# Halves of the heads in batch 0's attention, and a list of units over eight steps instead of four

## The chip, the cores and the metric

The kernel runs on one core of one Trainium2 chip. What counts is the time of one execution on the device in microseconds. Three runs of the kernel before took 1492.59 to 1493.74 us, 1492.81 in the median. One further execution was profiled. It took 1490.52 us, and the span that its trace covers is 1488.7 us. The mean clock granted to TensorE over that span is 0.992 of full speed. The engines are called PE (TensorE), DVE (VectorE), ACT (ScalarE), POOL (GpSimd) and SP (SyncE, which issues the DMAs here).

## The reference

Eight batches and eight heads attend twice, first with 32 packed queries over the keys, then with all queries over the packed result. Two feed-forward networks follow.

```python
# q, k, v: (8, 8, 576, 64), p: (8, 8, 32, 64); w_a, w_b: (512, 1536); w_out: (1536, 512)
# second network: w_in (512, 2048), w_out (2048, 512)
def sm_attn(qq, kk, vv):
    s = 0.125 * np.matmul(qq, kk.transpose(0, 1, 3, 2))
    a = np.exp(s - np.max(s, axis=-1, keepdims=True))
    a = a / (np.sum(a, axis=-1, keepdims=True) + 1e-09)
    return np.matmul(a, vv)
p_packed = sm_attn(p, k, v)
out = sm_attn(q, p_packed, p_packed)
x = out.transpose(0, 2, 1, 3).reshape(4608, 512)
x = (x @ w_a) * (x @ w_b) @ w_out
h = x @ w_in2
x = (h * np.clip(h + 3.0, 0.0, 6.0) / 6.0) @ w_out2
```

## The kernel before

**Numbers.** Every FP32 product of the two networks is made of three matmuls over high and low parts (`mm3`, L90 to L92): high by high, high by low, low by high. A high part is a copy of a value in the matmul's type, made on ACT as a rule, and the low part is the difference, made on DVE or POOL. All weights come as 64-bit words and are turned into FP32 in pieces of 128x512: `ld` loads a piece, `sq` (L112) and `lw` (L115, the low words, written into the destination) run on ACT, `a0` (L119), `a1` (L123) and `a2` (L128) on DVE, `a3` (L131) merges on POOL, and `st` stores the result to DRAM for later use. `sq 3` is that operation of piece 3. A scratch array of a piece is `cv_ap` in the trace, its raw words `f64p`, and the finished weights of a step `rab`.

**Phase 1** runs in 48 steps: 4 groups of two batches by 12 steps, one for each block of 128 columns of the first network's inner dimension. The attention's second product is never formed by itself: step t multiplies the packed attention `lhs` of both batches into the weights (`pw`, 16 matmuls, L524). `pwh` on ACT (L532) and `pwl` on DVE (L536) split its two PSUM banks into `pw_hi` and `pw_lo`. Then `ab t b h` multiplies them with the second softmax `at_hi`, `at_lo` (12 matmuls into two PSUM tiles, once for each of two batches and two halves of the tokens). `aba` (ACT, L564) copies one of the two tiles out, `abg` (DVE, L570) multiplies it with the other to `g`, `gh` (ACT, L577) and `gl` (POOL, L581) split it. Every third step makes 16 `y` units ready, of 9 matmuls each, which multiply three steps of `g` by `wo_hi`, `wo_lo` (`woh` on ACT, `wol` on POOL) and add the result to an accumulator.

**Attention units of a batch**, in order: `s1` (first scores, 16 matmuls over two banks, L214), `s1c` (copy to `ex`), `mx` (maximum), `ex` (exponential, L240), `et` and `et2` (transposes on PE, L246 and L259), `etc` and `et2c` (their copies on ACT, L251 and L264), `rs`, `pv` (40 matmuls, L280), `pp` (scaling, L287), `bd` (transpose) and `bdc` (copy into `lhs`). Then the second scores `s2`, their 32x32 transposes `s2c` (L309), `mx2`, `su2`, `ex2`, `sm2`, `mu2` (L333), `tr2` (L337), `ath` (ACT, L346) and `atl` (L350, on POOL, `atld` on DVE). The two digits behind a name are the batch and `c`, one of two arrays that hold four heads each; `s1`, `s1c`, `s2` and `s2c` take the half of the tokens instead. A `d` or `p` at the end of a name puts the unit on DVE or POOL.

**The order.** Every engine runs its instructions in the order in which the program issues them. For the first `TO` steps this order is the text `OPENING`, unit by unit. From step `TO` on a loop issues a step's `pw`, its `ab` units and `y` units with background units spread between them: the attention of later batches, from number `N_BG` of their list on, and the conversions. Units put off with `later` come due after a number of ticks; `DUE` holds what is still put off when the list ends. PSUM has eight banks: three tagged `att`, two `y`, three `ab`. In the opening a unit that asks for a bank takes them in rotation, from the token `bank` on as its own tag says. The second phase (the second network) is not touched.

Of the kernel before, what the change touches and what calls it, by code (L numbers as in the profile page):

```python
# [44 lines left out]
v 1 0, s2 0 0, ex 1 0, lw 2, ld, q 1 0, s2 0 1, s2c 0 0, s2c 0 1, a1 2, mx2 0 0, su2 0 0, mx2 0 1, q 1 1, a2 2, ex 1 1,
ex2 0 0, et 1 1, su2 0 1, etc 1 1, et 1 0, et2 1, ex2 0 1, ld, a0 3, etc 1 0, et2c 1, sm2 0 0, pv 1, a3 2, sm2 0 1, mu2 0 0,
rs 1, mu2p 0 1, sq 3, pp 1, tr2 0 0, tr2 0 1, bd 1, lw 4, bdc 1, a1 3, s2 1 0, s2c 1 0, ld, pw 0, st 1, lw 3, a0 4, st 2,
ath 0 1, ath 0 0, atl 0 1, a1 4, pwh 0 0, atl 0 0, pwl 0 0, pwh 0 1, pwl 0 1, s2 1 1, ab 0 0 0, s2c 1 1, mx2 1 0, mx2 1 1,
su2 1 0, a2 3, su2d 1 1, ab 0 0 1, a3 3, aba 0 0, ex2 1 0, abg 0 0, ex2 1 1, gh 0 0, sm2 1 0, pw 1, gl 0 0, aba 0 1, sq 4,
pwh 1 0, ld, abg 0 1, sm2 1 1, a2 4, mu2 1 1, gh 0 1, pwh 1 1, pwl 1 0, pwl 1 1, mu2p 1 0, a3 4, tr2 1 1, ab 1 0 0, ab 1 0 1,  # L50
aba 1 0, tr2 1 0, gl 0 1, abg 1 0, ys 0 1, ath 1 1, ath 1 0, ld, ys 0 0, atld 1 0, lw 5, aba 1 1, atl 1 1, gh 1 0, ab 0 1 0,
gl 1 0, sq 5, aba 0 2, abg 1 1, a0 5, ab 0 1 1, p 2, k 2 1, abg 0 2, v 2 0, st 3, a1 5, bank, gh 1 1, ld, gl 1 1, aba 0 3,
gh 0 2, abg 0 3, gl 0 2, gh 0 3, a0 6, a2 5, gl 0 3, sq 6, k 2 0, q 2 0, s1 2 0, s1c 2 0, s1 2 1, ys 0 3, v 2 1, a3 5, a1 6,
st 5, lw 6, s1c 2 1, ys 1 1, a2 6, mx 2 0, a0 7, mx 2 1, a1 7, sq 7, ld, ys 1 0, lw 7, sq 8, pw 2, a2 7, a3 6, ys 0 2,
ex 2 0, pwh 2 1, q 2 1, st 4, et 2 0, pwh 2 0, a0 8, pwl 2 0, lw 8, ex 2 1, a3 7, etc 2 0, pwl 2 1, a1 8, a2 8, lw 9,
ab 1 1 0, a3 8, aba 1 2, a0 9, woh 0 0, et 2 1, ld, abg 1 2, sq 9, gh 1 2, ld, etc 2 1, a1 9, ab 1 1 1, aba 1 3, abg 1 3,
wol 0 0, a2 9, et2 2, p 3, st 7, ab 2 0 0, ld, woh 0 1, st 8, wol 0 1, aba 2 0, st 6, gl 1 2, sq 10, abg 2 0, a3 9, rs 2,
et2c 2, a0 10, ys 1 2, woh 1 0, pv 2, pp 2, ld, a1 10, woh 1 1, bd 2, bdc 2, a0 11, pw 3, wol 1 0, gh 2 0, gl 2 0, st 9,
lw 10, ab 2 0 1, a2 10, pwh 3 0, lw 12, aba 2 1, ab 2 1 0, aba 2 2, ld, ys 2 0, abg 2 1, a3 10, gh 2 1, pwh 3 1, wol 1 1,
a1 11, pwl 3 0, woh 2 0, abg 2 2, wol 2 0, sq 12, woh 2 1, st 10, gh 1 3, pwl 3 1, a0 12, wol 2 1, ld, ld, gl 2 1, gl 1 3, y,  # L60
a1 12, ys 2 1, k 3 0, gh 2 2, gl 2 2, sq 11, a2 11, lw 11, a3 11, ab 2 1 1, ys 2 2, aba 2 3, a2 12, y, s2 2 0, y, ys 1 3,
abg 2 3, st 11, gh 2 3, a3 12, lw 13, ld, s2c 2 0, a0 13, ab 3 0 0, k 3 1, ab 3 0 1, ld, s2 2 1, s2c 2 1, aba 3 0, abg 3 0,
y, gh 3 0, a1 13, sq 13, gl 3 0, pw 4, gl 2 3, ys 2 3, v 3 1, aba 3 1, pwh 4 1, abg 3 1, v 3 0, a0 14, lw 14, y, a1 14,
# [1186 lines left out]
```

## Time and profile before

| | |
|---|---|
| median of three runs | 1492.81 us (1492.59 to 1493.74) |
| profiled execution | 1490.52 us |
| its span | 1488.7 us |
| PE busy | 1446.8 us, 97% of the span |
| DVE busy | 1089.7 us, 73% |
| ACT busy | 714.9 us, 48% |
| POOL busy | 561.6 us, 38% |
| DMA | 231 GB/s in the mean |

An engine's busy time counts the instructions that the profile times, not its waits. The idle time before an instruction is put down to the engine and line whose semaphore came last. A share of busy time is a mean over stretches with different limits, so the stretches have to be looked at one by one. The start of the span stands apart: only there the conversion of weights, the first attention units and the first steps compete for DVE, ACT and POOL at once.

### The profile page before, as it was taken

To read this page: it belongs to the slowest core of one execution; us is meant where nothing else is said; L and a number is where in the kernel's file an instruction comes from. 1 tells how busy PE (TensorE), PEld (TensorE's weight loads), DVE (VectorE), ACT (ScalarE), POOL (GpSimd) and SP (SyncE) were. 2 spreads that over 40 slices of the span, in tenths; PEclk is the share of its full clock that TensorE was granted. 3 is DMA by queue.
4 is the path that set the end of the run, shared out by engine and by line. 5 is a ranking of instruction groups with operands and counts; after the bars stand their busy time and mean duration, and the time that the engine had idled before them with its cause. 6 is when DMAs were issued, how large, how long until landed. Compare 5 with 4: busy or idle time off the path is not lost.

```text
span 1488.7 us, 29158 instructions
## 1 busy us (share of the span) xinstructions
PE 1446.8 (97%) x11416; PEld 1378.3 (93%) x11416; DVE 1089.7 (73%) x1728; ACT 714.9 (48%) x1421; POOL 561.6 (38%) x552
## 2 busy tenths in 40 slices
PE   4898999999999999999999999999999999999998
PEld 2687898999999899999999999999999999999998
DVE  5987785677865678535447788788788788878777
ACT  4665655565555555454423443453443343353333
POOL 2676555575554655645630324024024022111000
PEclk8899999999999999999999999999999999999999
DMA  9675545655577543855428768778768777867755
GB/s 313 222 232 169 174 155 204 225 195 181 180 245 229 168 167 134 272 200 185 178 75 333 286 248 314 270 265 309 283 232 298 290 257 291 298 221 292 267 217 184
DMA packets 120106, 344.54 MB, mean 231 GB/s; under 512 B 11424, under 2 KB 50336, under 8 KB 108192
## 3 DMA queue, kind: packets, MB, share of 16 engines
q1 hardware_dynamic: 119968, 342.67, 65.1%
q8 instruction: 90, 1.47, 0.4%
q14 instruction: 48, 0.39, 0.1%
HBM read 280.76 MB, written 61.87 MB: 230 GB/s over the span
## 4 chain that ended last, share of the span: by engine, by line
PE 87%; DVE 4%; DMA 3%; POOL 2%; issue 2%; ACT 1%; SPq 0%; DVEq 0%; POOLq 0%; ACTq 0%
PE o L91 8%; PE o L92 8%; PE o L90 8%; PE y L90 7%; PE y L92 6%; PE y L91 6%; PE ab L90 6%; PE ab L92 6%; PE ab L91 6%; PE pw L524 3%; DMA f64p<-in_wab 2%; PE s L214 1%; DMA w<-w2d 1%; POOL wo_lo L510 1%; DVE pw_lo L536 1%
## 5 line engine op out<-in xcount | busy, mean ns | idle before, releaser
L90 PE MATMUL ab<-at_hi,pw_hi 128*128 128x288 f32 x768 | 233.2, 304 | 2.7 <-DVE g L570 1.3
L90 PE MATMUL y<-g_hi,wo_hi 128*128 128x288 f32 x768 | 231.8, 302 | 1.3 <-ACT wo_hi L506 0.7
L92 PE MATMUL ab<-at_hi,pw_lo 128*128 128x288 f32 x768 | 228.6, 298 | 2.3 <-DVE pw_lo L536 2.3
L91 PE MATMUL ab<-at_lo,pw_hi 128*128 128x288 f32 x768 | 228.3, 297 | 0.0
L91 PE MATMUL y<-g_lo,wo_hi 128*128 128x288 f32 x768 | 227.1, 296 | 0.5 <-POOL g_lo L581 0.5
L92 PE MATMUL y<-g_hi,wo_lo 128*128 128x288 f32 x768 | 226.7, 295 | 0.6 <-POOL wo_lo L510 0.6
L91 PE MATMUL o<-ol,wo 128*128 128x384 f32 x672 | 226.9, 338 | 0.2 <-DVE ol L980 0.2
L92 PE MATMUL o<-oh,wo 128*128 128x384 f32 x672 | 226.8, 337 | 0.0
L90 PE MATMUL o<-oh,wo 128*128 128x384 f32 x672 | 225.5, 336 | 0.0
L581 POOL TENSOR_TENSOR g_lo<-g,g_hi 128x288 fp32r<-128x288 f32 x192 | 164.3, 860 | 137.1 <-ACT g_hi L577 133.1
L570 DVE TENSOR_TENSOR g<-a,ab 128x288 f32<-128x288 f32 x192 | 85.9, 447 | 117.0 <-PE ab L92 82.8
L90 PEld LDWEIGHTS y<-g_hi,wo_hi 128*128 128x128 f32 x768 | 144.6, 188 | 19.3 <-DVE acc L614 7.2
L90 PEld LDWEIGHTS ab<-at_hi,pw_hi 128*128 128x128 f32 x768 | 145.8, 190 | 17.3 <-issue 7.2
L718 POOL TENSOR_TENSOR yl_B<-raw_y,yh_B 128x384 fp32r<-128x384 f32 x36 | 50.1, 1412 | 262.8 <-PE h_7y L92 228.7
L92 PEld LDWEIGHTS ab<-at_hi,pw_lo 128*128 128x128 f32 x768 | 145.9, 190 | 3.0 <-DVE pw_lo L536 3.0
L91 PEld LDWEIGHTS ab<-at_lo,pw_hi 128*128 128x128 f32 x768 | 146.0, 190 | 0.1
L92 PEld LDWEIGHTS y<-g_hi,wo_lo 128*128 128x128 f32 x768 | 144.6, 188 | 1.1 <-POOL wo_lo L510 1.1
L91 PEld LDWEIGHTS y<-g_lo,wo_hi 128*128 128x128 f32 x768 | 144.6, 188 | 0.7 <-POOL g_lo L581 0.7
L564 ACT COPY a<-ab 128x288 f32<-128x288 f32 x192 | 76.6, 399 | 125.3 <-PE ab L92 124.6
L577 ACT CAST g_hi<-g 128x288 fp32r<-128x288 f32 x192 | 83.5, 435 | 91.5 <-DVE g L570 91.3
L91 PEld LDWEIGHTS o<-ol,wo 128*128 128x128 f32 x672 | 126.2, 188 | 0.7 <-DVE ol L980 0.5
L90 PEld LDWEIGHTS o<-oh,wo 128*128 128x128 f32 x672 | 126.1, 188 | 0.0
(434 smaller groups left out, 3414.5 us busy)
## 6 DMA issues: line engine op xcount, KB each, us to landing
wo<-wo2d SPq DMA_DIRECT2D x84, 1024.0 KB, 5.7
w<-w2d SPq DMA_DIRECT2D x47, 1280.0 KB, 8.1
w<-w2d SPq DMA_DIRECT2D x47, 512.0 KB, 4.9
rab<-wabf SPq DMA_DIRECT2D x36, 512.0 KB, 5.8
f64p<-in_wo SPq DMA_DIRECT2D x28, 512.0 KB, 3.7
w2d<-w SPq DMA_DIRECT2D x8, 1792.0 KB, 6.7
f64p<-in_wab SPq DMA_DIRECT2D x24, 512.0 KB, 4.9
k<-in_kT SPq DMA_DIRECT2D x16, 576.0 KB, 6.8
```

The lines of the kernel that those rows point to most:

```text
L90: pe.matmul(ps, lhsT=l_hi, rhs=r_hi, start=first, stop=False, skip_group_check=skip)
L91: pe.matmul(ps, lhsT=l_hi, rhs=r_lo, start=False, stop=False, skip_group_check=skip)
L92: pe.matmul(ps, lhsT=l_lo, rhs=r_hi, start=False, stop=last, skip_group_check=skip)
L214: pe.matmul(ps[c][o, :SH], lhsT=lhsT[r, q, :], rhs=kq_t[n, b, q // 2][r, q % 2, ts], start=True, stop=True)
L510: pool.tensor_sub(ol, ro_t[t][:, c * 256:(c + 1) * 256], f32(oh))
L524: pe.matmul(ps[c][o, b, :], lhsT=l[r, b, q, :], rhs=w[r, q, :], start=True, stop=True)
L536: dve.tensor_sub(lo[:, c], ps[c], f32(hi[:, c]))
L564: act.copy(a, ab_t[t, r][0])
L570: dve.tensor_mul(g32, a, p1)
L577: act.copy(g_t[t, r][0], g_t[t, r][2])
L581: pool.tensor_sub(lo, g32, f32(hi))
L718: pool.tensor_sub(lo[:, k], get(n)[:, k], f32(hi[:, k]))
```

## The change

The list covers steps 0 to 7 instead of 0 to 3, and its first part is written in another order. Of the entries that are common to both, many change places; line numbers of the kernel rise with the added functions (L214 becomes L233, L246 L265 and so on).

```diff
-TO, N_BG = 4, 23
-DUE = [[2, ('ys', 3, 3)]]
+TO, N_BG = 8, 43
+DUE = [[1, ('gh', 7, 3), ('gl', 7, 3), ('yslater', 7, 3)]]
 OPENING = """
-ld, k 0 0, p 0, lw 0, k 0 1, p 1, k 1 1, s1 0 0, v 0 1, s1c 0 0, s1 0 1, ld, s1c 0 1, mx 0 0, a0 0, mx 0 1, k 1 0, v 0 0,
...
+k 0 0, ld, p 0, k 0 1, s1x 0 0 0, ld, lw 0, s1x 0 0 1, s1x 0 1 0, p 1, s1x 0 1 1, s1cx 0 0 0, a0 0, s1cx 0 0 1, a1 0, wm,
+s1cx 0 1 0, s1cx 0 1 1, mx 0 0, ex 0 0, k 1 1, mx 0 1, wm, k 1 0, ex 0 1, v 0 0, v 0 1, wm, q 0 0, s1 1 1, et2x 0 1, et 0 1,
...
+    def heads1(ps, lhsT, n, b, h, c):
+        ts = slice(h * SH, (h + 1) * SH)
+        for q in range(4):
+            r, o = slice(64 * c, 64 * c + 64), slice(NP * q, NP * q + NP)
+            pe.matmul(ps[o, :SH], lhsT=lhsT[r, q, :], rhs=kq_t[n, b, q // 2][r, q % 2, ts], start=True, stop=True)
+
+    def s1x(b, h, c):
+        state(b)["s1", h, c] = ps = bank(f"s1_{b}{h}{c}")
+        heads1(ps, p_t[b], "k", b, h, c)
...
+    def et2x(b, c):
+        z = state(b)
+        z["pe", c] = ps = bank(f"et2{b}{c}")
+        for i in range(2):
+            pe.transpose(ps[:TR, i * P:(i + 1) * P], z["ex"][c][:, 3 * P + i * TR:3 * P + (i + 1) * TR], ident)
...
+    def pvx(b, c):
+        z = state(b)
+        z["pv", c] = ps = bank(f"pv{b}{c}")
+        for i in range(5):
+            r = P if i < 3 else TR
+            for q in range(4):
+                pe.matmul(ps[NP * q:NP * q + NP, :64], lhsT=z["et"][c][:r, i, NP * q:NP * q + NP],
+                          rhs=v_t[b, c][:r, i, 64 * q:64 * q + 64], start=i == 0, stop=i == 4)
...
+    def bdx(b, c):
+        z = state(b)
+        z["pb", c] = ps = bank(f"bd{b}{c}")
+        m = 64 if c == 0 else P
+        pe.transpose(ps[:m, :P], z["pp"][:, :m], ident)
...
+    def s2x(b, h, c):
+        z = state(b)
+        z["s2", h, c] = ps = bank(f"s2_{b}{h}{c}")
+        heads1(ps, z["bd"], "q", b, h, c)
...
+    def wm():
+        ps = bank(f"wm{n_bank[0]}")
+        for _ in range(5):
+            pe.transpose(ps[:, :P], ident, ident)
```

`s1x`, `s1cx`, `et2x`, `et2cx`, `rsx`, `pvx`, `ppx`, `bdx`, `bdcx`, `s2x` and `s2cx` are the units of the same name without the x, cut to one `c`, each with a PSUM bank of its own. The list uses them for batch 0 alone; batch 1 keeps the old units. `wm` transposes `ident` five times into a bank that nothing reads; the list holds six. Further added functions, `mx2h` to `atlh` by halves of the tokens and `pwb`, `pwhb`, `pwlb` by batch, are in no list.

On ACT, in the opening of batch 0: `ex` is the exponential, `rab` the low words, `cv_sqp` the squares, `et` the copies of the transposes. Before:

```order
L240 ACTIVATE ex_116,sm_150<-ex_116,nb_136 128x576
L112 ACTIVATE cv_sqp_0_156<-f64p_0_89 128x512
L115 ACTIVATE rab_95<-f64p_1_130 128x512
L240 ACTIVATE ex_117,sm_164<-ex_117,nb_142 128x576
L112 ACTIVATE cv_sqp_1_166<-f64p_1_130 128x512
L251 COPY et_169<-et_152 128x384
L251 COPY et_183<-et_171 128x384
L264 COPY et_169<-et_186 96x256
```

Now, at the same place:

```order
L330 ACTIVATE ex_123,sm_142<-ex_123,nb_140 128x576
L330 ACTIVATE ex_127,sm_158<-ex_127,nb_148 128x576
L131 ACTIVATE cv_sqp_0_193<-f64p_0_91 128x512
L341 COPY et_207<-et_203 128x384
L134 ACTIVATE rab_104<-f64p_1_102 128x512
L341 COPY et_210<-et_187 128x384
L263 COPY et_207<-et_197 96x256
L263 COPY et_210<-et_184 96x256
```

The two exponentials follow each other, and the low words of the second piece stand between the copies.

On DVE, the rows up to the first `pw_lo`: `at` (L337, after L427) are batch 0's last transposes, `cv_ap` the conversion, `t` (L309, after L399) the transposes of batch 1's second scores. Before:

```order
L337 STREAM_TRANSPOSE at_423<-t_317 128x576
L337 STREAM_TRANSPOSE at_425<-t_319 128x576
L123 SCALAR_TENSOR_TENSOR cv_ap_1_354<-f64p_1_303,cv_ap_1_354 128x512
L309 STREAM_TRANSPOSE t_443<-s_100_433 128x288
L309 STREAM_TRANSPOSE t_445<-s_101_434 128x288
L119 TENSOR_SCALAR cv_ap_0_471<-f64p_0_352 128x512
L123 SCALAR_TENSOR_TENSOR cv_ap_0_471<-f64p_0_352,cv_ap_0_471 128x512
L536 TENSOR_TENSOR pw_lo_468<-pw_0_449,pw_hi_467 128x512
L536 TENSOR_TENSOR pw_lo_468<-pw_1_450,pw_hi_467 128x512
```

Now:

```order
L142 SCALAR_TENSOR_TENSOR cv_ap_1_386<-f64p_1_283,cv_ap_1_386 128x512
L138 TENSOR_SCALAR cv_ap_0_474<-f64p_0_335 128x512
L427 STREAM_TRANSPOSE at_476<-t_351 128x576
L427 STREAM_TRANSPOSE at_478<-t_337 128x576
L142 SCALAR_TENSOR_TENSOR cv_ap_0_474<-f64p_0_335,cv_ap_0_474 128x512
L399 STREAM_TRANSPOSE t_517<-s_100_507 128x288
L399 STREAM_TRANSPOSE t_519<-s_101_508 128x288
L672 TENSOR_TENSOR pw_lo_503<-pw_0_484,pw_hi_502 128x512
L672 TENSOR_TENSOR pw_lo_503<-pw_1_485,pw_hi_502 128x512
```

Two conversion instructions stand in front of batch 0's transposes instead of behind them, and one directly behind.

On DVE around the `pw_lo` of step 6, with `g` the products of step 5. Before:

```order
L570 TENSOR_TENSOR g_5_0_1693<-a_0_1691,ab_01_1684 128x288
L119 TENSOR_SCALAR cv_ap_2_1703<-f64p_2_1423 128x512
L123 SCALAR_TENSOR_TENSOR cv_ap_2_1703<-f64p_2_1423,cv_ap_2_1703 128x512
L128 SCALAR_TENSOR_TENSOR cv_ap_2_1703<-cv_sqp_2_1700,cv_ap_2_1703 128x512
L119 TENSOR_SCALAR cv_ap_0_1741<-f64p_0_1504 128x512
L570 TENSOR_TENSOR g_5_1_1763<-a_1_1761,ab_11_1754 128x288
L536 TENSOR_TENSOR pw_lo_1728<-pw_0_1709,pw_hi_1727 128x512
L536 TENSOR_TENSOR pw_lo_1728<-pw_1_1710,pw_hi_1727 128x512
```

Now:

```order
L734 TENSOR_TENSOR g_5_0_1779<-a_0_1737,ab_01_1730 128x288
L142 SCALAR_TENSOR_TENSOR cv_ap_2_1719<-f64p_2_1350,cv_ap_2_1719 128x512
L147 SCALAR_TENSOR_TENSOR cv_ap_2_1719<-cv_sqp_2_1697,cv_ap_2_1719 128x512
L672 TENSOR_TENSOR pw_lo_1762<-pw_1_1744,pw_hi_1761 128x512
L427 STREAM_TRANSPOSE at_1807<-t_1222 128x576
L734 TENSOR_TENSOR g_5_1_1809<-a_1_1804,ab_11_1772 128x288
L138 TENSOR_SCALAR cv_ap_0_1834<-f64p_0_1542 128x512
L142 SCALAR_TENSOR_TENSOR cv_ap_0_1834<-f64p_0_1542,cv_ap_0_1834 128x512
L147 SCALAR_TENSOR_TENSOR cv_ap_0_1834<-cv_sqp_0_1740,cv_ap_0_1834 128x512
L672 TENSOR_TENSOR pw_lo_1762<-pw_0_1743,pw_hi_1761 128x512
```

The half 1 of `pw_lo` stands in front of `g_5_1`, the half 0 five rows behind the first.

## Rows read from the trace of the kernel before

**Rows 1.** The page: engine, busy us, share of the span, instructions.

```profile
PE 1446.8 (97%) x11416; PEld 1378.3 (93%) x11416; DVE 1089.7 (73%) x1728; ACT 714.9 (48%) x1421; POOL 561.6 (38%) x552
```

**Rows 2.** Stretch, length, busy PE, PEld, DVE, ACT, POOL, clock, DMA, GB/s.

```profile
22.00:60.00 38.00, 26.60 (x310) 19.68 (x310) 34.14 (x67) 19.84 (x43) 21.17 (x18) 0.73 0.73 249
60.00:120.00 60.00, 54.75 (x585) 48.04 (x586) 54.57 (x84) 42.53 (x102) 42.30 (x38) 1.00 0.69 227
120.00:140.00 20.00, 16.09 (x144) 13.12 (x144) 13.09 (x22) 11.43 (x27) 14.91 (x15) 0.91 0.54 175
140.00:1488.00 1348.00, 1339.56 (x10227) 1292.54 (x10225) 982.23 (x1542) 631.56 (x1231) 481.14 (x477) 1.00 0.65 231
```

**Rows 3.** Time line, batch 0: start, us, engine, operation, [wait before it <-releaser].

```profile
8.99 2.15 PE L214 MATMUL s<-k,p 64*32 64x288 f32 x24 [0.22 <-DMA k<-in_kT]
...
14.43 0.67 ACT L115 ACTIVATE rab<-f64p 128x512 int32<-128x512 uint16 x1 [0.33 <-DMA f64p<-in_wab]
15.01 0.76 ACT L240 ACTIVATE ex<-ex,nb 128x576 f32<-128x576 f32 x1
16.33 1.00 ACT L251 COPY et<-et 128x384 f32<-128x384 f32 x2
16.61 1.06 PE L259 MATMUL et<-ident,ex 128*96 128x128 f32 x4
17.71 0.64 ACT L264 COPY et<-et 96x256 f32<-96x256 f32 x2 [0.37 <-PE et L259]
...
19.70 1.80 PE L280 MATMUL pv<-v,et 128*32 128x64 f32 x80
21.57 0.48 DVE L287 TENSOR_SCALAR pp<-pv,rs 128x64 f32<-128x64 f32 x2 [4.40 <-PE pv L280]
...
25.83 0.87 PE L246 MATMUL et<-ident,ex 128*128 128x128 f32 x6 [1.77 <-ACT ex L240]
```

**Rows 4.** Time line: a conversion on DVE alone and beside POOL's `at_lo`.

```profile
13.66 0.68 DVE L123 SCALAR_TENSOR_TENSOR cv_ap<-f64p,cv_ap 128x512 uint32<-128x512 uint32 x1
...
36.80 3.00 POOL L350 TENSOR_TENSOR at_lo<-at,at_hi 128x576 fp32r<-128x576 f32 x2 [2.08 <-ACT at_hi L346]
...
38.54 1.80 DVE L123 SCALAR_TENSOR_TENSOR cv_ap<-f64p,cv_ap 128x512 uint32<-128x512 uint32 x1
```

**Rows 5.** Time line of DVE in front of the second `pw_lo`.

```profile
48.67 0.63 DVE L128 SCALAR_TENSOR_TENSOR cv_ap<-cv_sqp,cv_ap 128x512 f32<-128x512 f32 x1
49.21 0.74 DVE L333 TENSOR_TENSOR t<-t,sm 128x576 f32<-128x576 f32 x1
49.87 1.28 DVE L536 TENSOR_TENSOR pw_lo<-pw,pw_hi 128x512 fp32r<-128x512 f32 x2
```

**Rows 6.** DVE's `at_lo`, and its waits (us, times, longest), 44 to 60 us.

```profile
53.54 1.28 DVE L350 TENSOR_TENSOR at_lo<-at,at_hi 128x576 fp32r<-128x576 f32 x1
...
DVE g L570 <- PE ab L92: 1.5, 2, 0.8
```

**Rows 7.** Time line around `ab 4 0`, each matmul by itself.

```profile
100.41 0.29 PE L90 MATMUL y<-g_hi,wo_hi 128*128 128x288 f32 x1
...
103.33 0.44 DVE L570 TENSOR_TENSOR g<-a,ab 128x288 f32<-128x288 f32 x1
...
103.99 0.30 PE L90 MATMUL ab<-at_hi,pw_hi 128*128 128x288 f32 x1
```

**Rows 8.** Time line around the `pw` of step 6.

```profile
122.97 1.07 PE L524 MATMUL pw<-rab,lhs 64*32 64x256 f32 x24 [1.63 <-POOL rab L131]
124.09 1.08 ACT L532 CAST pw_hi<-pw 128x512 fp32r<-128x512 f32 x2 [1.80 <-PE pw L524]
...
127.51 0.46 DVE L570 TENSOR_TENSOR g<-a,ab 128x288 f32<-128x288 f32 x1 [1.97 <-ACT a L564]
128.71 0.71 PE L214 MATMUL s<-k,p 64*32 64x288 f32 x14 [2.28 <-DVE pw_lo L536]
```

**Rows 9.** Busy time and clock by stretch, columns as in rows 2.

```profile
130.00:134.00 4.00, 4.00 (x21) 4.00 (x20) 2.05 (x5) 3.27 (x8) 2.99 (x4) 0.58 0.57 189
```

More of the change, by code (lines that the diff above doesn't have):

```diff
@@ L45 @@
[L45 to L63, printed above, removed]
@@ L338, in tr2, with half, mx2h, su2h @@
         at32_t[b, c] = a
+    def half(x, h):
+        return x[:, 9 * h:9 * h + 9]
+    def mx2h(b, c, h):
+        z = state(b)
+        z["mx"][c, h] = att.tile([P, 9], F32, tag=f"mxh{h}", name=f"mxh{b}{c}{h}", bufs=2)
+        dve.tensor_reduce(z["mx"][c, h], half(z["t"][c], h), axis=AX.X, op=ALU.max)
+    def su2h(b, c, h, on=None):
+        t, m = half(state(b)["t"][c], h), state(b)["mx"][c, h]
+        (on or pool).tensor_tensor(t, t, m.unsqueeze(2).to_broadcast([P, 9, NP]), op=ALU.subtract)
+    def ex2h(b, c, h):
+        t = half(state(b)["t"][c], h)
+        act.activation(t, t, AF.Exp, scale=QK_SCALE)
+    def sm2h(b, c, h):
+        z = state(b)
+        z["sm2", c, h] = s = att.tile([P, 9], F32, tag=f"smh{h}", name=f"smh{b}{c}{h}", bufs=2)
+        dve.tensor_reduce(s, half(z["t"][c], h), axis=AX.X, op=ALU.add)
+        dve.tensor_scalar_add(s, s, 1e-9)
+        dve.reciprocal(s, s)
+    def mu2h(b, c, h, on=None):
+        t, s = half(state(b)["t"][c], h), state(b)["sm2", c, h]
+        (on or dve).tensor_tensor(t, t, s.unsqueeze(2).to_broadcast([P, 9, NP]), op=ALU.mult)
+    def tr2h(b, c, h):
+        if h == 0:
+            at32_t[b, c] = att.tile([P, S], F32, tag="at32", name=f"at32{b}{c}", bufs=2)
+        dve.transpose(at32_t[b, c][:, h * SH:(h + 1) * SH], half(state(b)["t"][c], h).rearrange("p j n -> p (j n)"))
+    def athh(b, c, h):
+        if b not in at_t:
+            at_t[b] = (
+                main.tile([P, 2, S], F32R, tag="at_hi", name=f"at_hi{b}", bufs=3),
+                main.tile([P, 2, S], F32R, tag="at_lo", name=f"at_lo{b}", bufs=3),
+            )
+        ts = slice(h * SH, (h + 1) * SH)
+        act.copy(at_t[b][0][:, c, ts], at32_t[b, c][:, ts])
+    def atlh(b, c, h, on=None):
+        hi, lo = at_t[b]
+        ts = slice(h * SH, (h + 1) * SH)
+        (on or pool).tensor_sub(lo[:, c, ts], at32_t[b, c][:, ts], f32(hi[:, c, ts]))
     def ath(b, c):
@@ L536, in pwl, with pwb, pwhb, pwlb @@
         dve.tensor_sub(lo[:, c], ps[c], f32(hi[:, c]))
+    def pwb(t, b):
+        l = lhs[t // NM1]
+        w = rab_t[t].rearrange("p (q n) -> p q n", q=4)
+        if t not in pw_t:
+            ps = [bank(f"pw{t}_{c}").rearrange("p (b n) -> p b n", b=2) for c in range(2)]
+            pw_t[t] = [
+                main.tile([P, 2, 2, 256], F32R, tag="pw_hi", name=f"pw_hi{t}", bufs=2),
+                main.tile([P, 2, 2, 256], F32R, tag="pw_lo", name=f"pw_lo{t}", bufs=2), ps,
+            ]
+        ps = pw_t[t][2]
+        for q in range(4):
+            for c in range(2):
+                r, o = slice(64 * c, 64 * c + 64), slice(NP * q, NP * q + NP)
+                pe.matmul(ps[c][o, b, :], lhsT=l[r, b, q, :], rhs=w[r, q, :], start=True, stop=True)
+    def pwhb(t, b, c):
+        hi, lo, ps = pw_t[t]
+        act.copy(hi[:, c, b], ps[c][:, b])
+    def pwlb(t, b, c):
+        hi, lo, ps = pw_t[t]
+        dve.tensor_sub(lo[:, c, b], ps[c][:, b], f32(hi[:, c, b]))
+    def wm():
+        ps = bank(f"wm{n_bank[0]}")
+        for _ in range(5):
+            pe.transpose(ps[:, :P], ident, ident)
     def pw_unit(t):
```

80 lines of the change are left out of this document (75 added, 5 removed).

## The prediction

> **What bounds the kernel now.** I read the page's busy times first, then busy time by stretch, then the time lines of the stretches in which PE waits. PE is busy 1446.8 of 1488.7 us [rows 1], so at most 41.9 us of waiting can go, plus what PE loses at its lower clock. The stretches say where it lies [rows 2]: from 140 us on PE is busy 1339.6 of 1348 us, so whatever moves PE earlier in the first 140 us reaches the end unchanged, and nothing behind that point has much to give. From 22 to 60 us PE waits 11.4 us, from 60 to 120 us 5.3, from 120 to 140 us 3.9. DVE is busy 34.1 of 38 us in the first of these and 54.6 of 60 in the second: up to 120 us PE mostly waits for what DVE has not yet done. So in each part I ask what brings DVE forward, or what takes away a stall of PE at 120 to 130 us. Work that only fills a gap of PE is worth nothing by itself.
>
> **The change, part by part.** The DVE, ACT and POOL work is the same set but for two moves (C, D); PE gets 30 transposes more, the six `wm`. Only batch 0 goes through the new half units: batch 1 still uses `s1`, `et2`, `pv` and `s2`. DVE's rows from number 246 on are identical in both orders, so nothing behind step 8 is touched. The new OPENING leaves the same conversions, loads and attention units done at step 8 as the loop did.
>
> *A, up to batch 0's `pp`.* Before, ACT reads low words (0.67, after 0.33 of waiting for a transfer) between the two exps, and the second starts at 15.01; now it follows the first, over 1 us earlier [rows 3]. But PE runs 15 `wm` transposes in front. Four transposes take 1.06 there, 0.27 each. The last score unit ends at 11.1 (8.99+2.15), `wm` then near 15.1; the 16 matmuls of `s1 1 1`, at the rate of 24 in 2.15, near 16.5; batch 0's ten transposes near 19.2. ACT's copies follow: 0.50, low words 0.67, 0.50, and 0.64 for the last two, to 21.5; `pv` 1.80 and one scaling 0.24 end `pp` at 23.5, against 22.05 before (21.57+0.48): +1.5. Where PE has reached its higher rate by then (six transposes in 0.87 at 25.83), the transposes behind `wm` and `s1 1 1` take half: `pp` near 21.5, -0.6. The score matmuls of one half now stand in fours behind each other instead of alternating with the other half's; no row shows that order. Side by side they cost nothing; one after the other, 24 matmuls take up to 2.15 more. I take 0, nearest to the row where the rate is already high (25.83), for `wm` keeps PE busy from 9 us on; range -0.6 to +2.2.
>
> *B, from `pp` to the first `pw_lo`.* DVE has the same instructions between the two, but a merge (`cv_ap`, 38.54) moves in front of batch 0's last transposes. It took 1.80 beside POOL's two `at_lo` (36.80, 3.00 for both), against 0.68 for the same form at 13.66 with POOL idle [rows 4]. Free of them it gives 1.1. But another merge now stands right behind the transposes, just where `at_lo` starts. I take -0.6, the middle (range 0 to -1.1). [...]
>
> *C, first to second `pw_lo`.* `mu2` of one half of batch 1 (0.74 at 49.21) goes from DVE to POOL, and a product of the conversion (0.63 at 48.67) goes behind `pw_lo`, which started at 49.87 and can start near 48.67 [rows 5]: -1.2. If POOL is late with `mu2`, the next transposes wait for it: range -1.2 to 0.
>
> *D, batch 1's second `at_lo` goes from POOL to DVE,* 1.28 long [rows 6]. DVE waits 1.5 us for `ab` in the same step; that covers it: 0, uncovered +1.3.
>
> *E, `pw_lo` of step 4* stands seven to eight rows further back on DVE, around the last `g` of step 3. Before, that `g` ran 103.33 to 103.77, and `ab 4 0` started at 103.99; three `y` units in front of it take from 100.41 to 103.99, 1.2 each, and one of them now comes later [rows 7]. So PE is at `ab 4 0` at 102.8, about 1 us before its `pw_lo`: +0.8, as its first two matmuls don't need it; range 0 to +2.
>
> *F, the stalls around `pw 6`.* PE waits 1.63 us at 122.97 for `rab` and 2.28 at 128.71, where `s1 3 0` needs a PSUM buffer that `pw_lo` frees. `pw_lo` itself stands behind a `g` that waited 1.97 for ACT [rows 8]. Now one half of `pw_lo` stands in front of that `g`, right behind a conversion: `pw_hi` from 124.09, half of 1.08, and the 0.64 of C's form give 125.3, before PE has run the twelve matmuls of `ab 5 0 1` behind `pw 6` (122.97+1.07, then 1.6). So 2.3 us go. The first stall stays: it ends with the same conversion, with the same work in front of it. F is -2.3; range 0 to -2.3.
>
> *G, the clock behind them.* [...]
>
> Sum: 0 - 0.6 - 1.2 + 0 + 0.8 - 2.3 - 1.7 = -5.0 us. The profiled execution took 1490.5 us, 1.8 over its span; the median of the runs, 1492.8, lies 2.3 above it. That gives 1485.5 for an execution like the profiled one and **1487.8 us** for the median.
>
> **The rivals.** (1) *The late stall comes back in another place.* ACT's and POOL's orders in steps 4 to 7 are new throughout. If `s1 3 0` still waits, for `pw_hi` behind two casts of `g` on ACT, F and G fall out and A to E leave -1.0: 1491.8. Against it: those casts have their input before `pw 6` ends.
>
> [...]
>
> (3) *Slower: `pw_lo` comes too late for `ab`.* It stands further back in DVE's order at steps 4, 5, 6 and 8. If DVE runs 3 us behind PE there, `ab 4 0` and `ab 8 0` each wait 3 us and lose 1.7 to the clock, as in rows 9: 9.4 in place of E's 0.8, in sum +3.6: 1496.4. It decides from 5.8 us of such stalls on. For it: E's margin is already negative. Against it: behind `pw 5` five `y` and three `ab` units stand in front of `ab 5 0`, 10.8 us at 1.2 and 1.6 each.
>
> (4) *The early gain does not pass on.* DVE's head start can end in its own waits for PE: it idles 5.4 of the 60 us up to 120 [rows 2]. Then B and C are lost and E costs 2: 2.0 - 4.0 = -2.0, 1490.8.
>
> **How the numbers follow.** Forecast 0.48; (1) 0.15; (2) 0.10; (3) 0.13; (4) 0.14. A difference under 0.2%, 3.0 us, cannot be told from none. Faster by more: nine tenths of the forecast, (2), and 0.08 out of (1) and (4): 0.61. Slower by more: (3) and 0.01 from A's upper end: 0.14. Between: 0.25. Without (2) the terms reach -6.9 at best; the likeliest case's own range is 1484 to 1491. With half of (2) and most of (3) the range is 1481.5 to 1495.5.
>
> **What would show it.** In the profile after: `pp` of batch 0 ends at 21.5 to 23 us; the second `pw_lo` pair starts near 48 instead of 49.87; no wait of `s` for `pw_lo` behind `pw 6` and a granted clock of 1.00 there; one wait of `ab` for `pw_lo` of about 1 us near 101 us; waiting of PE from 120 to 140 us under 2. I am wrong in A to C if the first `pw_lo` comes no earlier than before, in F and G if PE's waits from 120 to 250 us do not shrink, and in the whole if the stretch from 22 to 60 us runs at 1.00.

## The result and the profile after

The changed kernel takes 1477.37 us in the median (1475.91 to 1478.94), the kernel before 1492.70 in the runs beside it. The ratio is 0.990 (0.9887 to 0.9912): 15.3 us less, three times what was forecast, and 4 us below the range. The profiled execution took 1476.74 us with a span of 1475.0, against 1490.52 and 1488.7.

The page of the kernel after, columns as in [rows 1]:

```profile
PE 1443.9 (98%) x11447; PEld 1377.0 (93%) x11447; DVE 1090.0 (74%) x1728; ACT 713.5 (48%) x1422; POOL 562.1 (38%) x552
```

DVE, ACT and POOL are as busy as before [rows 1], and the span is shorter. PE waits 31.1 us (1475.0 - 1443.9) instead of 41.9. The stretches of the kernel after, columns and bounds as in [rows 2]:

```profile
22.00:60.00 38.00, 28.12 (x369) 20.07 (x354) 35.62 (x72) 24.90 (x55) 22.99 (x19) 0.87 0.73 247
60.00:120.00 60.00, 58.51 (x631) 53.21 (x630) 57.54 (x90) 45.39 (x110) 46.17 (x43) 1.00 0.76 257
120.00:140.00 20.00, 20.00 (x186) 18.68 (x185) 17.66 (x33) 11.96 (x29) 15.40 (x16) 1.00 0.55 188
140.00:1475.00 1335.00, 1324.62 (x10084) 1277.36 (x10083) 970.99 (x1517) 621.33 (x1210) 474.31 (x469) 1.00 0.65 231
```

In the second stretch PE waited 5.3 us before and waits 1.5 now, in the third 3.9 and nothing, and the granted clock is 1.00 in both. In the first the clock rose from 0.73 to 0.87.

How far the kernel after leads at the same work is read best from the starts of `pw`. These are their starts in the profiled executions, in us, with those of the first four experiments beside them. At pw 0 the old order has one `s2` more behind it; at pw 2, 4, 6 and 9 PE has done the same work but for `wm`.

| kernel | pw 0 | pw 2 | pw 4 | pw 6 | pw 9 |
|---|---|---|---|---|---|
| before | 36.59 | 60.97 | 92.51 | 120.70 | 173.64 |
| after | 32.46 | 54.98 | 83.44 | 111.35 | 157.75 |
| `early_part` | 32.65 | 55.56 | 84.06 | 111.94 | 166.06 |
| `late_part` | 36.55 | 60.93 | 92.46 | 120.80 | 168.90 |
| `steps01_part` | 33.07 | 56.91 | 87.68 | 115.88 | 168.77 |
| `steps23_part` | 37.30 | 61.50 | 90.92 | 118.80 | 172.90 |

The lead of after over before is 6.0 us at pw 2, 9.1 at pw 4, 9.4 at pw 6 and 15.9 at pw 9. So it is made in three places: up to pw 2, between pw 2 and pw 4, and around pw 6. Executions of one order differ, though. The kernel after, `early_part`, `steps01_part` and `pw_lo6_back` (all explained below) have the same order up to pw 2, and reach it between 54.98 and 56.91. A difference of under 2 us between two of these starts says little by itself. The way from pw 2 to pw 4 is steadier: 28.5 us in the three of them that have the new order there, 30.8 in `steps01_part` and 31.5 before. Later this one execution gives back 2 us (a wait of `y` for an accumulator of 1.01 at 367.8 us is the largest piece), and the medians differ by 15.3.

**Batch 0 and 1.** The time line of the kernel after in the opening answers to [rows 3]:

```profile
10.95 3.34 PE L700 MATMUL wm<-ident 128*128 128x128 f32 x15
...
12.51 0.78 ACT L330 ACTIVATE ex<-ex,nb 128x576 f32<-128x576 f32 x1 [0.77 <-DVE nb L325]
...
13.35 0.78 ACT L330 ACTIVATE ex<-ex,nb 128x576 f32<-128x576 f32 x1
...
14.21 0.72 PE L233 MATMUL s<-k,p 64*32 64x288 f32 x16
...
19.26 0.28 DVE L284 TENSOR_SCALAR pp<-pv,rs 128x64 f32<-128x64 f32 x1 [0.28 <-PE pv L277]
```

`pp` of batch 0 ends at 19.5 (19.26+0.28) instead of 22.05 [rows 3]. The first and the second pair of `pw_lo` follow on DVE, in the time line of the kernel before at 40.27 and 49.87 [rows 5], in that of the kernel after at 36.24 and 44.97:

```profile
40.27 1.27 DVE L536 TENSOR_TENSOR pw_lo<-pw,pw_hi 128x512 fp32r<-128x512 f32 x2
```

```profile
36.24 1.25 DVE L672 TENSOR_TENSOR pw_lo<-pw,pw_hi 128x512 fp32r<-128x512 f32 x2
...
44.97 1.22 DVE L672 TENSOR_TENSOR pw_lo<-pw,pw_hi 128x512 fp32r<-128x512 f32 x2
```

But a larger wait stands between `pp` and the first `pw_lo`, which no row of the prediction shows. It heads PE's waits of the kernel before from 20 to 36 us (engine, line, waited for: us, times, longest):

```profile
PE pv L280 <- ACT et L251: 4.2, 1, 4.2
PE et L246 <- ACT ex L240: 1.8, 1, 1.8
PE bd L292 <- DVE pp L287: 1.7, 2, 1.0
```

The time line of the kernel before around it (`t` are the second scores, L318 is `su2`, L322 `ex2`, L264 `et2c`):

```profile
27.50 2.72 POOL L318 TENSOR_TENSOR t<-t,mx 128x576 f32<-128x576 f32 x2 [3.49 <-DVE mx L314]
...
28.69 0.68 ACT L322 ACTIVATE t<-t 128x576 f32<-128x576 f32 x1 [2.91 <-POOL t L318]
...
30.25 0.68 ACT L322 ACTIVATE t<-t 128x576 f32<-128x576 f32 x1 [0.51 <-POOL t L318]
...
31.20 0.64 ACT L264 COPY et<-et 96x256 f32<-96x256 f32 x2
...
31.36 2.36 PE L280 MATMUL pv<-v,et 128*32 128x64 f32 x80 [4.21 <-ACT et L251]
```

It reads from the bottom up. PE's `pv` of batch 1 waits 4.2 us for copies of its transposes on ACT. One of these stands between batch 0's two `ex2`, the others behind both, and the two `ex2` wait 2.9 and 0.5 us for the two `su2`, one after the other on POOL. The transposes themselves were done at 27 us. The same place in the kernel after (L408 is `su2`, L412 `ex2`, L341 the copies):

```profile
25.83 1.54 POOL L408 TENSOR_TENSOR t<-t,mx 128x576 f32<-128x576 f32 x1 [4.34 <-DVE mx L404]
...
27.05 0.94 DVE L408 TENSOR_TENSOR t<-t,mx 128x576 f32<-128x576 f32 x1
...
27.40 1.30 ACT L412 ACTIVATE t<-t 128x576 f32<-128x576 f32 x2 [1.83 <-POOL t L408]
...
28.73 0.86 ACT L341 COPY et<-et 128x384 f32<-128x384 f32 x2
...
29.64 0.58 PE L370 MATMUL pv<-v,et 128*32 128x64 f32 x25 [1.61 <-ACT et L341]
```

One `su2` runs on DVE beside the other on POOL, both `ex2` follow without a gap, and `pv` waits 1.6.

**Around pw 6.** The time line of the kernel after answers to [rows 8]:

```profile
111.35 1.26 PE L660 MATMUL pw<-rab,lhs 64*32 64x256 f32 x32
...
112.83 0.59 ACT L668 CAST pw_hi<-pw 128x512 fp32r<-128x512 f32 x1
...
113.46 0.69 DVE L672 TENSOR_TENSOR pw_lo<-pw,pw_hi 128x512 fp32r<-128x512 f32 x1
...
114.32 0.72 PE L233 MATMUL s<-k,p 64*32 64x288 f32 x16
...
115.12 0.46 DVE L734 TENSOR_TENSOR g<-a,ab 128x288 f32<-128x288 f32 x1 [0.28 <-PE s L233]
```

All 32 matmuls of `pw 6` run in one piece (before, 24 of them waited 1.63 for `rab`), and `s1 3 0` does not wait (before, 2.28 for `pw_lo`).

### The profile page after: what moved, and what is told of

It reads as the page before. It is cut to its first block, busy times and chain, and to the rows that moved or that the text cites. A ratio compares the mean times of both kernels' runs of the same rounds, so it can differ in the third digit from the quotient of the medians.

```text
span 1475.0 us, 29209 instructions
## 1 busy us (share of the span) xinstructions
PE 1443.9 (98%) x11447; PEld 1377.0 (93%) x11447; DVE 1090.0 (74%) x1728; ACT 713.5 (48%) x1422; POOL 562.1 (38%) x552
## 4 chain that ended last, share of the span: by engine, by line
PE 90%; DVE 4%; DMA 2%; ACT 1%; issue 1%; POOL 1%; SPq 0%; DVEq 0%; ACTq 0%; POOLq 0%
PE o L110 8%; PE o L111 8%; PE o L109 8%; PE y L109 7%; PE y L111 7%; PE y L110 7%; PE ab L109 6%; PE ab L111 6%; PE ab L110 6%; PE pw L660 3%; PE s L233 1%; DMA w<-w2d 1%; DMA wo2d<-wop_lo 1%; PE pv L370 1%; DMA k<-in_kT 0%
```

## The experiments

An interval is that of the ratio to the kernel before. Differences are between medians, in us. A negative one is to the kernel before in the runs beside it; the kernel after is at -15.3. The kernel after did not run beside these kernels, so where one is called slower than it, two medians from different runs are compared.

**Where the gain is made: the list in parts.**

```diff
# early_part: after, list cut to the old list's units, in the new order
+TO, N_BG = 4, 23      # from step 4 on the loop, as before
# steps01_part: the new list up to `pw 2`, then the old order, then the loop
# steps23_part: the old list up to `pw 2`, then the new order, then the loop
# late_part: the old list, then the new list's further units in their order
+TO, N_BG = 8, 43
```

> The new order and units for steps 0 to 3 alone (the list is cut to the units that the old list held, kept in the new order; from step 4 on the loop issues the work as before). Theory (the gain is made in three places that add up, read from the lead of the changed kernel's pw over before's: 3.1 us at pw 1, 6.0 at pw 2, 8.3 at pw 3, 9.1 at pw 4): 9 us faster than before, 1483.7; PE still waits about 4 us around pw 6, and its clock still falls behind these waits. Rival A (an early lead is given back where the loop takes over): under 4 us faster, 1489 or more, with more waiting than before from 85 to 140 us. Rival B (the lead removes the stalls around pw 6 by itself, since the conversions come earlier too): 13 to 16 us faster, no wait of s for pw_lo behind pw 6.

Measured: 1483.96, -9.0 (0.992 to 0.9956). As the theory had it. Both stalls around pw 6 are there (1.54 and 2.27 us).

> The old list for steps 0 to 3 with the old units, then the new list's remaining units in their new order for steps 4 to 7. Theory: only the stalls around pw 6 (1.6 and 2.3 us) and the half clock behind them (1.7) go, and what the same work gained between pw 6 and pw 9 in the changed kernel, 6.4 us in all: 1486.3. Rival A (the explicit order of steps 4 to 7 only works on top of the early lead, as its conversions would come too late by 9 us): no gain, 1491 or more, with new waits for rab or pw_lo at pw 5 to pw 8. Rival B (nearly the whole gain is made here): 12 us or more.

Measured: 1487.45, -5.5 (0.9955 to 0.9977). The theory, somewhat smaller: the lead is 0 up to pw 6 and 4.7 at pw 9.

> The new order up to pw 2 (the halves of batch 0, the six wm, steps 0 and 1), then the old list's order and the loop. Theory: the lead at pw 2 in the changed kernel, 5.5 to 6 us, passes on: 1487. Rival A (DVE, which is nearly always busy up to 120 us, has its lead from steps 2 and 3): 2 us or less. Rival B (the lead grows by itself behind pw 2, because the second fall of the clock, at 51.7 us before, is gone): 8 us or more.

Measured: 1487.84, -5.1 (0.9951 to 0.9975). The theory; 4.1 us of lead at pw 2, 4.9 at pw 9.

> The old order up to pw 2, then the new order of what the old list holds behind it, then the loop. Theory: the lead grows by 3.1 us between pw 2 and pw 4, where PE's waits for ex, rab, pw_lo and pp of batch 2 shrink from 5.4 to 3.1 us: 3 us faster, 1489.7. Rival A (these waits shrink only because DVE arrives earlier): no change, 1492 or more. Rival B: a part of the stall at pw 6 goes too, 5 us or more.

Measured: 1493.28, +0.4 (0.9987 to 1.0008). No change: Rival A by its number, but not by its reason. The new order does shorten the way from pw 2 to pw 4, from 31.5 us to 29.4. Behind the stalls at pw 6, which it leaves, the next pw comes 19.73 us after the second piece of pw 6 instead of 18.49, with a granted clock of 0.83 from 120 to 140 us instead of 0.91. Before pw 2, where the order is the old one, this execution happened to be late too: its first `pw` started 0.7 later. So -9.0 of the opening and -5.5 of the late steps add up to -14.5 of the 15.3. Within the opening, steps 2 and 3 are worth 3.9 behind the new earlier steps (-5.1 in `steps01_part`, -9.0 in `early_part`), with both stalls around pw 6 still there, and nothing that could be told behind the old ones. Why that is so is not shown: the longer way behind pw 6 is that of one execution.

**What of the opening does it: `wm`, halves, engines.**

```diff
# no_wm: wm() takes its bank, without the transposes
-        for _ in range(5):
-            pe.transpose(ps[:, :P], ident, ident)
# no_halves: each pair of x units is the old unit, where its last half stood
-pvx 0 1, ... pvx 0 0, ...
+pv 0, ...
# old_engines
-su2d 0 1, mu2p 0 0, mu2p 1 1, atld 1 1
+su2 0 1, mu2 0 0, mu2 1 1, atl 1 1
# more_wm: 5 wm in front of `et 1 1`, 2 of `pv 1`, 1 of `bd 1`
```

> The changed kernel without the 30 transposes of wm; each wm still takes its PSUM bank in the rotation, so everything else stands as it did. Theory (PE reaches its higher rate at 14.2 us because it had worked without a pause from 7.4 us on, the last 3.3 us of it on wm): without them the scores, the ten transposes and the pv of batch 0 run at the lower rate (16 score matmuls in 1.5 us instead of 0.72 at 14.2 us), pp of batch 0 ends about 1 to 1.5 us later than 19.5, and the whole takes 1 to 1.5 us more: 1478.6. Rival A (transposes don't bring PE to its higher rate, it would have come there anyway, and the 3.3 us stand in front of useful work): the same or up to 1.5 us faster, 1476 to 1477.4. Rival B (the whole gain of the opening is the clock's): 4 us slower or more.

Measured: 1477.88 (0.988 to 0.9914). `pp` of batch 0 ends at 20.4 instead of 19.5, the first `pw_lo` starts at 37.6 instead of 36.2, but in the medians 0.5 is left, which cannot be told from nothing. Neither the theory's 1 to 1.5 us nor Rival A is excluded by it.

> The changed kernel with batch 0 on the old units: a whole unit stands where the last of its two halves stood, wm and the order of the rest unchanged. Theory (the halves let the copies, the scalings and the second scores of one half start while PE works on the other; in the changed kernel pv of one half starts at 17.7 and its pp at 18.7, against 19.7 and 21.6 before): the first pw_lo comes about 1 us later than 36.2, 1478.5 in all. Rival A (the halves give nothing, the gain of the opening is that of the order and wm): 1477.4 within 0.5. Rival B (they give most of the opening's gain): 3 us slower or more.

Measured: 1476.76 (0.987 to 0.9905). Rival A: the halves give nothing. `pp` ends at 19.3, no later than with them.

> The changed kernel with four units back on the engines of before: su2 of batch 0's second half and atl of batch 1's second half on POOL, one mu2 each of batch 0 and batch 1 on DVE. Theory (the exchange of su2 and mu2 is what shortens the way from pp to the first pw_lo by 1.5 us, since before POOL ran both su2, the second only at 28.6, and DVE waited; and mu2 of batch 1 costs DVE 0.74 in front of the second pw_lo): first pw_lo about 1 us later than 36.2, second pair about 2 us later, 1479.4 in all. Rival A (DVE has so much else to do that it makes no difference): 1477.4 within 0.5. Rival B (POOL was the better place): faster, 1476.5 or less.

Measured: 1481.07 (0.9902 to 0.9931), 3.7 slower than the kernel after; all its runs lie above all of that kernel's. More than the theory (2.0), and of its kind: the first `pw_lo` starts at 38.66, and `pv` of batch 1 waits 3.95 for the copies on ACT.

> The changed kernel with eight wm more, where PE waits in front of batch 1's transposes (5 wm in a wait of 2.7 us at 22.9), in front of its pv (2, in 1.6 us) and in front of its bd (1, in 1.1 us). If a pause of PE is what lets the granted clock fall to half from 31.5 to 41.2 us, it now stays at 1.00 there. Theory (DVE is busy nearly all of that time and sets the end, so the clock is worth little): 0 to 1 us faster, 1476.9. Rival A (the half clock costs what PE works in it, 8 us at twice the time): 3 to 4 us faster, 1473.5, and the version that beats both. Rival B (the added transposes do not hold the clock and only stand in front of batch 1's work): up to 2 us slower.

Measured: 1479.67 (0.9891 to 0.9923), 2.3 slower than after, with overlapping intervals. The clock now holds from 28 to 40 us (1.00), but it falls earlier (0.66 from 18 to 28 us) and again later (0.57 from 40 to 44 us), and pw 0 comes at 34.57. The stretches of `more_wm`, columns as in [rows 2]:

```profile
18.00:28.00 10.00, 9.14 (x136) 5.49 (x136) 7.15 (x16) 4.71 (x13) 2.09 (x2) 0.66 1.06 364
28.00:40.00 12.00, 9.28 (x194) 7.45 (x193) 10.81 (x27) 6.53 (x13) 7.88 (x6) 1.00 0.80 296
40.00:44.00 4.00, 4.00 (x20) 4.00 (x20) 3.93 (x7) 2.30 (x5) 2.12 (x2) 0.57 0.00 0
```

Rival A did not come, but the added transposes also stand in front of work, so this run alone does not price the clock. What it is worth shows better where executions of the same order differ in it by chance. Up to pw 2 `early_part` and the kernel after have the same work in the same order; from 27 to 50 us the first has a clock of 0.93, the second of 0.78:

```profile
27.00:50.00 23.00, 17.03 (x239) 12.12 (x237) 21.90 (x46) 14.99 (x30) 15.84 (x13) 0.93 0.69 245
```

```profile
27.00:50.00 23.00, 17.55 (x236) 12.47 (x234) 22.17 (x46) 14.83 (x30) 15.51 (x13) 0.78 0.68 247
```

pw 1 comes 1.2 us earlier in the first (41.49 against 42.67), pw 2 no earlier (55.56 against 54.98). DVE is busy 22 of the 23 us in both. The two others of this order say the same: with a clock of 0.85 and 0.89 in these 23 us, `steps01_part` and `pw_lo6_back` have pw 1 at 42.23 and 41.07, pw 2 at 56.91 and 55.80. The lowest clock of the four has the earliest pw 2.

**Single pieces, alone.**

```diff
# before_moves: the old list, four units on the new engines
-mx2 0 1, q 1 1, a2 2, ... su2 0 1, ... mu2 0 0, ... mu2 1 1, ... atl 1 1
+mx2 0 1, q 1 1, su2d 0 1, a2 2, ... mu2p 0 0, ... mu2p 1 1, ... atld 1 1
# before_pw_lo6: the kernel before
-        later(1 if t >= NM1 else 2, seq((pwl, t, 0), (pwl, t, 1)))
+        later(1 if t >= NM1 or t == 6 else 2, seq((pwl, t, 0), (pwl, t, 1)))
# plain_units: no_halves and no_wm together, the wm dropped from the list
# late_moves: late_part with the four units on the new engines, each in its old place
```

> The kernel before with the four units on the engines of the changed kernel and nothing else: su2 of batch 0's second half on DVE, right behind its maximum, and atl of batch 1's second half on DVE; one mu2 each of batch 0 and batch 1 on POOL. Putting them back cost the changed kernel 3.7 us. Theory (what they bring is that ACT's copies of batch 1's transposes, which stand behind the second ex2, and so PE's pv, come earlier; but in the old order both su2 begin late, at 27.5 us, so that ex2 can come forward by 0.5 to 1 us only, and mu2 gives another 0.7 in front of the second pw_lo): 1 to 1.5 us faster, 1491.7. Rival A (the exchange is worth the same 3.7 us in the old order): 1489.3 or less. Rival B (DVE is the bound in the old order, so 0.94 and 1.28 more on it cost time): slower, 1493.5 or more.

Measured: 1492.27 (0.9984 to 1.0007), no difference that could be told. Neither rival in the medians. The interval reaches from 2.4 us faster to 1.0 slower, so it excludes Rival A, but neither the theory's 1 to 1.5 us nor a small loss.

> The kernel before with one edit: the two pw_lo of step 6 come due one tick earlier, which moves them on DVE in front of the g that waits for ACT, past two instructions of a conversion; nothing else moves. Theory (this place alone makes the stall of s1 3 0 and the half clock behind it): the wait of s for pw_lo, 2.3 us, goes, the granted clock from 130 to 134 us is 1.00, the first stall at pw 6 stays (1.6): 4 us faster, 1488.9. Rival A (the wait comes back as one for the conversion, which now stands behind pw_lo): under 2 us faster, with more waiting for rab at pw 7. Rival B (the clock falls all the same, as the first stall is enough): 2.3 us faster, 1490.5.

Measured: 1492.61 (0.9989 to 1.0012): nothing. `s` no longer waits for `pw_lo`, and the theory still fails: the wait has moved, to the conversion that now stands behind `pw_lo`. The time line of `before_pw_lo6` (`ro` are weights of the `y` units, L127 and L130 their conversion, L509 makes `wo_lo`), and two stretches, columns as in [rows 2]:

```profile
125.47 1.29 DVE L535 TENSOR_TENSOR pw_lo<-pw,pw_hi 128x512 fp32r<-128x512 f32 x2 [0.30 <-ACT pw_hi L531]
...
126.52 0.71 PE L213 MATMUL s<-k,p 64*32 64x288 f32 x16
...
126.67 1.01 DVE L127 SCALAR_TENSOR_TENSOR cv_ap<-cv_sqp,cv_ap 128x512 f32<-128x512 f32 x1
...
127.77 1.40 POOL L130 TENSOR_TENSOR ro<-cv_ap,ro 128x512 int32<-128x512 int32 x1 [0.62 <-DVE cv_ap L127]
...
130.97 1.18 POOL L509 TENSOR_TENSOR wo_lo<-ro,wo_hi 128x256 fp32r<-128x256 f32 x1
...
132.21 0.40 PE L91 MATMUL y<-g_hi,wo_lo 128*128 128x288 f32 x1 [1.75 <-POOL wo_lo L509]
```

```profile
120.00:131.00 11.00, 8.73 (x92) 6.43 (x90) 10.35 (x15) 7.20 (x17) 8.03 (x8) 1.00 0.62 200
131.00:137.00 6.00, 4.79 (x24) 4.80 (x25) 3.37 (x7) 2.56 (x6) 6.00 (x7) 0.72 0.65 204
```

A wait of 1.75 for `wo_lo` stands in the place of the 2.28, and the clock falls behind this one as well (0.72 from 131 to 137 us). POOL was slower there, too: `at_lo` (at 129.12) and `wo_lo` took 1.88 and 1.18 us, against 1.43 and 0.75 in the kernel before, while DVE ran a conversion of 1.80 (at 129.76). Rival A, for other weights than it named.

> The changed kernel with batch 0 on the old units and without wm: only the order and the four units on other engines are left of the change. Each of the two left out alone made no difference that could be measured (1476.8 without the halves, 1477.9 without wm). Theory (the order and the engines carry the whole gain): 1476.5 to 1478.5. Rival (each covers for the other, since both bring batch 0's pp forward): 1480 or more, with pp ending later than 20.4 us.

Measured: 1477.48 (0.988 to 0.9906). The theory: without halves and `wm` the kernel is as fast as the changed one, in the medians. In the traced execution pw 9 comes at 159.57, 1.8 later, no more than executions of one order differ at pw 2.

> The old list with the old units for steps 0 to 3, the four units on their new engines (each at its old place), and the new list's order for steps 4 to 7. The order of steps 4 to 7 on the old list took 1487.5. Theory (the opening's 9 us come from its order as a whole, of which the engines are a part that needs the earlier su2): 1486.5. Rival (late order and engines are most of the change): 1483 or less, so that the new order of the first steps would be worth 6 us at most.

Measured: 1486.66 (0.9941 to 0.9965), -6.0. The theory.

**What was still open.**

```diff
# su2_back: after
-su2d 0 1
+su2 0 1
# pw_lo6_back: after
-aba 5 1, pwl 6 1, tr2 2 1, abg 5 1,
+aba 5 1, tr2 2 1, abg 5 1, pwl 6 1,
# ex_apart: after
-ex 0 1, ... sq 0, ... lw 1
+sq 0, lw 1, ex 0 1
```

> The changed kernel with su2 of batch 0's second half back on POOL, where a merge of the conversion stands in front of it; nothing else moves. All four units back cost 3.7 us. Theory (this one unit is the cause: the second ex2 comes 2 us later, ACT's copies of batch 1's transposes stand behind it, and PE's pv waits about 4 us for them instead of 1.6): first pw_lo at about 38.5 instead of 36.2, 1480.5 in all. Rival A (mu2 of batch 1 in front of the second pw_lo and the other two make most of it): 1477.5 to 1478.5. Rival B (only all four together cost anything): 1477.4 within 0.5.

Measured: 1479.49 (0.9896 to 0.9924), 2.1 slower than after in the medians, with intervals that overlap. The time line of `su2_back` shows the place (L406 `su2`, L148 the merge, L410 `ex2`):

```profile
28.57 1.26 POOL L148 TENSOR_TENSOR rab<-cv_ap,rab 128x512 int32<-128x512 int32 x1
...
29.80 1.15 POOL L406 TENSOR_TENSOR t<-t,mx 128x576 f32<-128x576 f32 x1
...
30.98 0.68 ACT L410 ACTIVATE t<-t 128x576 f32<-128x576 f32 x1 [1.66 <-POOL t L406]
...
32.60 1.94 PE L368 MATMUL pv<-v,et 128*32 128x64 f32 x80 [4.22 <-ACT et L339]
```

The wait of 4.2 us of the kernel before is back from one unit, and the first `pw_lo` starts at 39.4. The theory, by its mechanism; of the 3.7 us of all four units this one is more than half in the medians. From the end of batch 0's `pp` to the first `pw_lo` it takes 19.5 us here and 19.0 in `old_engines`, where `su2` is on POOL, and 16.7 to 18.2 in the nine traced kernels that begin with the new order, or a variant of it, and have this `su2` on DVE.

> The changed kernel with the first of step 6's two pw_lo behind g_5_1 on DVE, where both stood before; the conversions keep their new, earlier places. In the changed kernel s1 3 0 doesn't wait at all. Theory (the prediction's step F holds where the conversion is early enough: the place of pw_lo decides when s1 3 0 gets its PSUM buffer): s1 3 0 waits again for 1 to 2 us, the clock falls behind it, 1479 to 1480.5. Rival A (what made that stall was that the g in front waited for ACT and everything was late; now g comes on time, and the place is worth nothing): 1477.4 within 0.7, no wait of s for pw_lo behind pw 6.

Measured: 1480.77 (0.9902 to 0.9927), 3.4 slower than after in the medians, though the intervals overlap a little. The time line of `pw_lo6_back`:

```profile
115.92 0.46 DVE L732 TENSOR_TENSOR g<-a,ab 128x288 f32<-128x288 f32 x1 [0.97 <-ACT a L726]
...
116.29 0.68 DVE L670 TENSOR_TENSOR pw_lo<-pw,pw_hi 128x512 fp32r<-128x512 f32 x1
...
117.12 0.71 PE L231 MATMUL s<-k,p 64*32 64x288 f32 x14 [1.34 <-DVE pw_lo L670]
```

The theory: with the conversions early, the place of this one `pw_lo` does bring the wait back. The clock did not fall here (1.00 from 112 to 120 us), but pw 7 comes 18.55 us after pw 6 instead of 16.58.

> The changed kernel with a square and the low words of the conversion between batch 0's two ex on ACT, as before; nothing else moves. Theory (the second ex starts 1.3 us later or more, as the low words wait for a transfer too, its transposes and pv follow, and pp of batch 0 ends near 20.8 instead of 19.5; the opening hands that on): 1 to 1.5 us slower, 1478.7. Rival A (DVE's work behind pp takes it up, as it did with the halves and wm): 1477.4 within 0.7. Rival B (the lead at pw 0 is all made here): 3 us slower or more.

Measured: 1477.05 (0.9881 to 0.9912). Rival A by its number. The second `ex` does start at 14.54 instead of 13.35, but the low words no longer stand between the copies of the transposes, where the changed kernel has them, and `pv` starts at 17.69 against 17.66.

## Why the prediction was wrong

The direction was right, and F and G named the right place. Of the missing 10 us, 8 belong to the opening, where A to E had -1.0 and `early_part` measures -9.0, and 2 to the steps behind it.

**A was mis-sized.** `pp` came 2.5 us earlier where 0 was taken, below the end of -0.6. The step charged the 15 `wm` with 4.0 us (11.1 to 15.1) in front of useful work; they took 3.34. `no_wm` shows that PE has nothing to do there: its `s1 1 1` waits for `k` until 13.49, while with `wm` it starts at 14.21 and runs in 0.72 instead of 1.22. Of the 2.5 us, `plain_units` keeps 1.8 by order alone (`pp` ends at 20.25), and its median is that of the changed kernel. So the other 0.7 cannot be told in the time. No run takes the 1.8 away, and what they are worth is not shown.

**B failed, by the count it began with.** "The same set but for two moves" was wrong: `su2` of batch 0's second half went from POOL to DVE and one `mu2` of batch 0 from DVE to POOL as well, four units in all. The way from `pp` to the first `pw_lo` shrank by 1.5 us, from 18.2 to 16.7, where -0.6 was taken. Over the four traces of each order up to there (16.7 to 18.2 and 18.1 to 19.1) it is 1.2 in the mean, at the end of the range. The merges themselves gave what was priced, if not as it was told: 0.65 and 1.80 before (at 35.85 and 38.54), 1.09 and 0.64 after (at 31.85 and 34.55), 0.7 less. The one that moved in front of the transposes is that of 35.85; that of 38.54 moved up to stand directly behind them. The deeper fault is the view. I read from 34.1 busy of 38 us [rows 2] that PE waits for DVE, and followed DVE. PE's largest wait there, 4.2 us, was for ACT, and through ACT for POOL, an engine busy 21.2 of 38 us in the same row. `su2_back` brings that wait back with one unit. A list of what PE waits for, from 20 to 36 us, says it in its first line. And the unit that paid was moved onto the busiest engine: DVE is busy 35.6 of the 38 us now. In the kernel after, the merge in front of the transposes takes 1.09 beside a `mu2` on POOL (31.23, 1.16). The merge that is left behind them takes 0.64 (34.55), though the first of POOL's two `at_lo` starts within it (34.75, 3.10 for both).

**C and D** came out near their prices: from first to second `pw_lo` 8.73 us instead of 9.60, -0.9 where -1.2 was taken, and no visible price for `at_lo` on DVE but a wait of 0.61 of `ab` for it.

**A term was missing for steps 2 and 3.** The stretch from 60 to 120 us has 5.3 us of waiting in [rows 2], and no term spoke of it, though the list gives batch 2's units a new order there. The lead grew by 3.1 us from pw 2 to pw 4. The trace of `steps23_part` shows 2.1 of that with no help from the opening, its median shows nothing; behind the new opening the two steps are worth 3.9 in the medians. Between the second `pw_lo` and pw 2 the lead grew by 1.1 more (4.9 to 6.0), for which there was no term either.

**E was too dear**: no `ab` waits for the `pw_lo` of step 4, and the lead stays 9.1 from pw 4 (83.44) to pw 5 (97.79 against 106.86). +0.8 should have been 0.

**F and G** were right in kind. F kept the first stall; it went too, since the new order has that merge done in time. From pw 6 to pw 9 the lead grew by 6.5 us, where F and G had 4.0 (2.3 + 1.7). No run shows G's -1.7, the last term of the sum, by itself: from 130 to 134 us the clock is 1.00 in the kernel after, against 0.58 before [rows 9], and the 6.5 us hold the two waits (1.63 and 2.28 us) and the clock together. But F named only half of the cause. Moving `pw_lo` alone gives nothing (`before_pw_lo6`), since the conversion that it passes is needed next. The new order puts the conversions earlier as well, and then the place of that `pw_lo` is worth 2.0 us in the trace and 3.4 in the medians (`pw_lo6_back`).

**The rivals.** (1), that the late stall comes back elsewhere, did not happen in the changed kernel; it is what happens to F's edit alone. (2), that `wm` holds the granted clock up from 22 to 60 us, gave the nearest time, 1483.9 (1487.8 less the 3.9 us that DVE waits there, 38 - 34.1 [rows 2]), by luck: the clock did rise from 0.73 to 0.87, but four executions of one order show no earlier pw 2 at a higher clock from 27 to 50 us. (3) and (4) did not happen: the early lead passed on, as -9.0 in the medians of `early_part`.

What stays open: the opening's order up to pw 2 is worth 5.1 us, of which the one `su2` carries about two. What carries the other three, and what of the order makes the 3.9 of steps 2 and 3, no run takes apart. No single piece that was tried besides (`wm`, halves, the two `ex` side by side) is worth a time that could be told, and what the exchange is worth in the old order (`before_moves`) lies inside the noise.
